# Matmuls on a constant tile in TensorE's waits of the first three attention items, and expert 1's weight split on ScalarE and VectorE

## The chip, the core and the metric

The kernel runs on one core of a Trainium2 chip. A core has TensorE (PE in the profile; its weight loads are PEld), VectorE (DVE), ScalarE (ACT), GpSimd (POOL) and SyncE (SP), each with its own instruction queue, and 16 DMA engines. The metric is the device time of one execution in microseconds; the number that counts is the median over several runs.

## The reference

Two parts in a row. Gated linear attention for 4 batches, 8 heads, 768 tokens, head size 48: `f = sigmoid(f_logit)`, and for every token `state = f * state + k (outer) v`, `y = q . state`. Its output is the input `x` (3072 tokens of 384) of a mixture of 8 experts with hidden size 1024:

```
P = np.exp(logits - logits.max())            # logits = x @ w_gate
for _ in range(8):
    P /= P.sum(1, keepdims=True) + 1e-09
    P /= P.sum(0, keepdims=True) + 1e-09
    P *= N / E
for e in range(E):
    out += P[:, e:e + 1] * (np.maximum(x @ w1[e], 0.0) @ w2[e])
```

Every token goes through every expert; the routing weights P need all logits, so all tokens, before they are known.

## The kernel before, in words

**Numbers.** Products are made in fp16 with each fp32 operand split in a high and a low half (names ending in h and l), so one product is three matmuls: high x high, high x low, low x high. A split is a cast to fp16 on ACT (the high half) and a subtraction on DVE or POOL (the low half).

**Stage 1, attention and raw experts (0 to about 420 us).** Attention is cut into 24 items of 128 tokens, 4 head pairs each. An item is a Python generator that yields between short groups of instructions. Its steps: load q, k and the gates (`q3`) and v (`vr`); sigmoid of the gates on ACT (`ft`); a reversed scan of their products on DVE (`r`); k times r (`km`); a second scan; q times it; high and low halves of k (`kb`), q (`qh`, `ql`) and v (`vh`, `vl`); k transposed (`ktp`, `kt`); scores (`aps`, masked into `am`, split into `ah`, `al`); outer products of k and v (`kvps`); the state (`st`, split into `sh`, `sl`) and the `carry` to the next item; the output (`yps`) and its split into the tokens `xh`, `xl`; and, two steps later, the gate logits (`lps`). An ordinary item (`item`, L615) transposes k by a DMA and uses POOL for q's product and k's low half. The first two (`early_item`, L495) transpose on PE and use DVE for both.

Between item steps PE runs a *filler*: experts 0 and 1 on tokens that are ready. For the first three blocks of 384 tokens it goes by tiles of 128 tokens (`moe_tile`, L417): twice 36 matmuls of 128 columns (`hps`), the halves `hh` on ACT and `hl` on DVE, then 24 matmuls of 384 columns (`yps`, the same name as the item's, told apart by its operands `w2h`, `w2l`). `raw_pairs` (L807) sets the order of tiles, expert 0 and expert 1 taking turns. `fill(n)` (L818) issues filler worth n units after each step of the loop; the table `FILL` gives n by step. One unit is one matmul of 384 columns, a third of one for 128. The loop over steps starts one new item every 8 steps, the first ordinary one `LEADS` steps in.

**Weights of experts 0 and 1.** `load` (L345) issues the DMA of one piece (4 of w1, 4 of w2 for each expert); later it splits it. Expert 0's pieces take one ACT operation (scale and cast, L360) and one on DVE (L362). Expert 1's go through `split_w` (L335): ACT scales in place (L340), ACT casts (L341), POOL subtracts (L342). Before the loop, a hand-written list of `go` and `fill` calls sets the order of item 0's steps, the loads and splits of expert 0, and the gate weights (`gate_weights`, L313).

**Stage 2, routing and conversion (about 420 to 514 us).** The filler goes on, 8 units a step. Beside it run the routing (`balance`, L941: 8 rounds of row and column sums on DVE with one small PE matmul `sk_c` a round) and the conversion of the tokens of each of 4 blocks to 15 sums and differences that the last stage multiplies (`convert`, L896; its casts on ACT, its subtractions on DVE). The next three conversions begin at steps 24, 48 and 64 of that loop (L1023); the last one's splits run on into the last stage.

**Stage 3, experts 2 to 7 (about 514 to 1563 us).** 48 periods of 15 slots (`period`, `SLOTS`). A slot is 6 matmuls into one of six PSUM banks `kb_A` to `kb_F`, with ACT copying (`cp`, L1164) and DVE adding (L1166, L1169) between them, and the second layer of the period before (`kyps`) fed in. A table `plan` holds side work by period and slot; among it the *checks* (`all_checks`, L1094): loads and maxima of all weights, then `guard` (L735) with samples of q, k (`qks`, 4 loads of 4 DMAs each) and v, then `verdict` (L775). Each call does one step of the checks, one to three of them a period.

**What sets the order.** `mm` (L278, its issue L279) chains all matmuls, so PE runs them in program order. `pin` (L270) chains an instruction behind the last pinned one of its engine. Nearly all work on DVE, ACT and POOL is pinned; the operations of `guard`, `verdict` and `partition_reduce` are not, so that the scheduler places them. SP issues DMAs in program order.

## Time and profile before

| what | value |
|---|---|
| runs (3), median | 1568.99 us |
| lowest, highest | 1566.51, 1572.23 us |
| the profiled execution's own time | 1571.83 us |
| its span in the trace | 1570.1 us |
| mean granted PE clock in it | 0.993 |
| PE busy | 1517.6 us (97%) |
| DVE busy | 1083.9 us (69%) |
| ACT busy | 780.4 us (50%) |
| POOL busy | 536.0 us (34%) |

The profile is of one execution. Matmuls overlap in it, so the time that one costs is the distance between the starts of two, not its own duration; a row may stand for several (x12). A wait names the engine and line that came last. PEclk or the clock column is the granted clock of PE as a share of full speed.

### The profile page before, as it was taken

How to read it: one execution, taken by the hardware profiler on the slowest of the kernel's cores; microseconds unless marked ns; L12 is line 12 of the kernel's file. 1: busy time of each engine (PE TensorE's matmuls, PEld its weight loads, DVE VectorE, ACT ScalarE, POOL GpSimd, SP SyncE). 2: the span in 40 equal slices, each digit the busy share in tenths (PEclk: the TensorE clock that was granted, in tenths of full speed). 3: DMA queues.
4: the chain of work that ended last, by engine and by line, in shares of the span. 5: the costliest groups of instructions: out<-in, count | busy, mean ns of one | idle time of the engine just before them, and what ended most of it. 6: DMA issues, size and time to landing. Idle time of an engine off the chain costs nothing.

```text
span 1570.1 us, 32383 instructions
## 1 busy us (share of the span) xinstructions
PE 1517.6 (97%) x13400; PEld 1107.5 (71%) x13400; DVE 1083.9 (69%) x1798; ACT 780.4 (50%) x1493; POOL 536.0 (34%) x668
## 2 busy tenths in 40 slices
PE   5799999999999999999999999999999999999998
PEld 4688886666655677777777777777777767777775
DVE  7687777887467866676767776666766675656654
ACT  5655555555334655554455554545444444445432
POOL 1643444343644512333333323223222222223211
PEclk9899999999999999999999999999999999999999
DMA  8355454542001212222222222121112220000011
GB/s 249 100 139 129 112 140 95 133 120 71 21 26 41 71 53 88 69 86 71 87 76 80 77 86 62 41 62 51 61 51 62 59 67 11 21 13 19 1 56 68
DMA packets 91501, 114.83 MB, mean 73 GB/s; under 512 B 52464, under 2 KB 68976, under 8 KB 91344
## 3 DMA queue, kind: packets, MB, share of 16 engines
q1 hardware_dynamic: 91344, 112.68, 25.3%
q8 instruction: 106, 1.74, 0.5%
q14 instruction: 51, 0.42, 0.1%
HBM read 88.41 MB, written 14.16 MB: 65 GB/s over the span
## 4 chain that ended last, share of the span: by engine, by line
PE 87%; DVE 6%; ACT 3%; DMA 1%; issue 1%; POOL 1%; SPq 0%; DVEq 0%; ACTq 0%; POOLq 0%
PE kyps L279 35%; PE yps L279 12%; PE hps L279 9%; PE kb_A L279 8%; PE kb_B L279 8%; PE kb_D L279 6%; PE kb_C L279 4%; PE kb_E L279 2%; PE kb_F L279 2%; PE kvps L279 1%; PE aps L279 1%; DVE hl L394 1%; DMA qks<-in_qkf_dram 1%; DMA vr<-in_vbd_dram 0%; ACT kb L647 0%
## 5 line engine op out<-in xcount | busy, mean ns | idle before, releaser
L1070 POOL TENSOR_TENSOR acc<-acc,yt 128x384 f32<-128x384 f32 x172 | 173.0, 1006 | 635.5 <-ACT yt L1069 635.5
L279 PE MATMUL kyps<-k2h,kh 128*128 128x384 f16 x1152 | 376.5, 327 | 0.0
L279 PE MATMUL kyps<-k2h,kl 128*128 128x384 f16 x1152 | 376.3, 327 | 0.0
L279 PE MATMUL kyps<-k2l,kh 128*128 128x384 f16 x1152 | 376.3, 327 | 0.0
L279 PEld LDWEIGHTS <-k1h 128*128 128x128 f16 x2880 | 281.4, 98 | 71.0 <-issue 0.2
L279 PEld LDWEIGHTS <-kh 128*128 128x128 f16 x2304 | 225.4, 98 | 104.5 <-issue 0.3
L1069 ACT ACTIVATE yt<-kyps,pes 128x384 f32<-128x384 f32 x172 | 99.8, 580 | 324.7 <-PE kyps L279 322.8
L279 PEld LDWEIGHTS <-k1l 128*128 128x128 f16 x1440 | 140.7, 98 | 69.2 <-issue 11.7
L1066 DVE SCALAR_TENSOR_TENSOR acc<-kyps,pes,acc 128x384 f32<-128x384 f32 x92 | 56.8, 618 | 171.8 <-PE kyps L279 171.8
L279 PEld LDWEIGHTS <-kl 128*128 128x128 f16 x1152 | 112.7, 98 | 44.8
L279 PE MATMUL yps<-w2l,hh 128*128 128x384 f16 x384 | 126.0, 328 | 5.1 <-POOL w2l L342 3.7
L1164 ACT ACTIVATE cp<-kb_A 128x512 f32<-128x512 f32 x144 | 86.0, 597 | 85.5 <-PE kb_A L279 83.6
L279 PE MATMUL yps<-w2h,hh 128*128 128x384 f16 x384 | 125.8, 328 | 2.6 <-ACT w2h L360 2.0
L279 PE MATMUL yps<-w2h,hl 128*128 128x384 f16 x384 | 125.9, 328 | 1.1 <-DVE hl L441 1.1
L279 PEld LDWEIGHTS <-w1h 128*128 128x128 f16 x1344 | 100.7, 101 | 36.5 <-ACT w1h L341 3.3
L1164 ACT ACTIVATE cp<-kb_B 128x512 f32<-128x512 f32 x144 | 87.0, 604 | 52.0 <-DVE kb_B L1166 52.0
L279 PEld LDWEIGHTS <-hh 128*128 128x128 f16 x768 | 74.6, 98 | 51.2 <-issue 6.4
L1169 DVE TENSOR_TENSOR cp<-kb_D,cp 128x512 f32<-128x512 f32 x144 | 98.9, 687 | 13.8 <-PE kb_D L279 12.8
L279 PE MATMUL hps<-xh,w1h 128*128 128x128 f16 (+1 forms) x672 | 86.3, 264 | 3.9 <-ACT w1h L341 3.0
L279 PE MATMUL hps<-xl,w1h 128*128 128x128 f16 (+1 forms) x672 | 86.4, 262 | 0.1
L394 DVE SCALAR_TENSOR_TENSOR hl<-hps,hh 128x384 f16<-128x384 f32 x80 | 43.9, 550 | 61.2 <-ACT hh L393 61.0
L279 PE MATMUL hps<-xh,w1l 128*128 128x128 f16 (+1 forms) x672 | 85.0, 261 | 0.0
(247 smaller groups left out, 3677.4 us busy)
## 6 DMA issues: line engine op xcount, KB each, us to landing
wm<-in_w_dram SPq DMA_DIRECT2D x64, 384.0 KB, 3.0
q<-in_qkf_dram SPq DMA_DIRECT2D x23, 672.0 KB, 5.1
vr<-in_vbd_dram SPq DMA_DIRECT2D x24, 384.0 KB, 3.6
ys<-yr SPq DMA_DIRECT2D x48, 192.0 KB, 2.3
k1r<-in_w_dram SPq DMA_DIRECT2D x24, 384.0 KB, 3.0
k2r<-in_w_dram SPq DMA_DIRECT2D x24, 384.0 KB, 3.0
yb<-ys SPq DMA_DIRECT2D x48, 192.0 KB, 2.3
out_dram<-acc SPq DMA_DIRECT2D x24, 192.0 KB, 1.9
```

The lines of the kernel that those rows point to most:

```text
L279: ins = (nc.tensor.transpose if transpose else nc.tensor.matmul)(**kw)
L394: held[0] = pin(nc.vector.scalar_tensor_tensor(out=tl, in0=ps, scalar=0.0, in1=th, op0=ALU.max, op1=ALU.subtract))
L1066: pin(nc.vector.scalar_tensor_tensor(out=y, in0=ps, scalar=p, in1=y, op0=ALU.mult, op1=ALU.add))
L1069: pin(nc.scalar.activation(out=yt, in_=ps, func=AF.Copy, scale=p))
L1070: pin(nc.gpsimd.tensor_tensor(out=y, in0=y, in1=yt, op=ALU.add))
L1164: pin(nc.scalar.activation(out=fresh(ev[2]), in_=bk, func=AF.Copy))
L1169: pin(nc.vector.tensor_tensor(out=fresh(ev[4]), in0=bk, in1=old, op=ALU.add if ev[2] == '+' else ALU.subtract))
```

## The change

Five things, in the order of the program.

1. **Early items.** `early_item` now makes items 0, 1 and 2 (ordinary items begin with number 3, `LEADS` 4 to 20). Its steps are shorter and in another order: the cast of v stands behind those of k and q, k's low half and q's low half have steps of their own, the output's matmuls go by operand (those that need only `vh` and `ah` first) in place of by head pair, and for items 1 and 2 the second chunk's transposes and outer products come ahead of them. At certain places `warm(n)` issues n matmuls of 512 columns of a constant tile (`ind`) by itself into a PSUM bank that nothing reads: 20 + 5 + 2 + 3 + 2 + 4 in item 0, 5 + 4 in items 1 and 2, 54 in all.
2. **Filler.** `raw_pairs` runs expert 0's three tiles of the first block, then expert 1's three, and takes turns only after that. `FILL` has seven rates in place of three.
3. **Weights.** All 8 pieces of expert 0 are requested ahead of item 1's data and of the gate weights. Expert 1's pieces are split like expert 0's: one ACT operation and one on DVE, at steps 18 to 22, while item 2 runs. `split_w` is gone, and with it POOL's part.
4. **Conversion.** Block 0's splits have one more step between them, the later conversions begin at steps 28, 48 and 62, and the last one's splits take every second slot of period 0.
5. **Checks.** The operations of `guard`, `verdict` and `partition_reduce` are pinned, and `guard` requests load n in the step in which it reduces load n - 1.

```diff
-LEADS = 4
-FILL = ((0, 6.5), (12, 6.3), (26, 9.1))
+LEADS = 20
+FILL = ((0, 12), (1, 4), (4, 6), (8, 0), (12, 6), (20, 9), (41, 8.6))
...
-        if e:
-            ws[e][k - 1].append(split_w(raw, e, j, k))
-            return
-        wh, wl = (wp0.tile(list(raw.shape), F16, name=f"w{k}{q}_0_{j}", tag=f"w{q}") for q in "hl")
+        wh, wl = ((wp1 if e else wp0).tile(list(raw.shape), F16, name=f"w{k}{q}_{e}_{j}", tag=f"w{q}") for q in "hl")
         scale = W1S if k == 1 else W2S
         pin(nc.scalar.activation(out=wh, in_=raw, func=AF.Copy, scale=scale))
         yield
         pin(nc.vector.scalar_tensor_tensor(out=wl, in0=raw, scalar=scale, in1=wh, op0=ALU.mult, op1=ALU.subtract))
...
+    def warm(n):
+        ps = bank([128, 512], f"wps{banks[0]}")
+        for _ in range(n):
+            mm(out=ps, lhsT=ind[:, 0:128], rhs=ind[:, 0:NB * C], start=True, stop=True)
...
+        if not i:
+            warm(20)
         transposed(0, 0)
+        yield
+        for rs, ks in heads:
+            pin(nc.vector.tensor_tensor(out=kb[rs, 1, :, ks], in0=km[rs], in1=kb[rs, 0, :, ks], op=ALU.subtract))
+        warm(5)
+        yield
+        pin(nc.vector.tensor_tensor(out=ql, in0=fl, in1=qh, op=ALU.subtract))
         transposed(1, 0)
+        if not i:
+            warm(2)
...
+        if i:
+            kv1 = outer(1)
+        warm(4)
...
-        for u in range(TILED):
+        for e in range(2):
+            for t in range(TT):
+                yield from moe_tile(e, 0, t)
+        for u in range(1, TILED):
             for t in range(TT):
                 for e in range(2):
                     yield from moe_tile(e, u, t)
...
+        at_steps(second[n], 4 + n, *((18, 18), (18, 18), (19, 19), (19, 19), (21, 21), (21, 21), (22, 22), (22, 22))[n])
...
+            if not b:
+                yield
...
-        if step in (24, 48, 64):
-            work.append(converts[{24: 1, 48: 2, 64: 3}[step]])
+        if step in (28, 48, 62):
+            work.append(converts[{28: 1, 48: 2, 62: 3}[step]])
...
-    at_slots(0, range(4, 15), converts[3])
-    at_slots(1, range(15), converts[3])
+    at_slots(0, range(4, 15, 2), converts[3])
+    at_slots(1, range(1, 15), converts[3])
```

and in `guard` (the loop over q, k and v in place of two loops):

```diff
+        for n in range(9):
+            now = (load_qk if n < 4 else load_v)(n % 4) if n < 8 else None
+            if before:
+                pin(nc.vector.tensor_reduce(out=before[1], in_=before[0], axis=AX.X, op=ALU.max, apply_absolute_value=True))
+            before = now
             yield
```

How the order of instructions moves is shown at three places. The first is SP's queue at the start. Names are tiles: `w1r_0_3` is the raw piece 3 of w1 of expert 0, `q3_1` and `vr_1` are item 1's data, `wgr` the gate weights. Before:

```order
L353 DMA w1r_0_3_169<-in_w1_dram 128x768
L315 DMA wgr_171<-in_wg_dram 128x384
L353 DMA w2r_0_0_173<-in_w2_dram 128x768
L353 DMA w2r_0_1_175<-in_w2_dram 128x768
L501 DMA q3_1_177<-in_qkf_dram 112x1536
L506 DMA vr_1_179<-in_vbd_dram 128x768
L353 DMA w2r_0_2_371<-in_w2_dram 128x768
```

After, in the same place:

```order
L343 DMA w1r_0_3_169<-in_w1_dram 128x768
L343 DMA w2r_0_0_171<-in_w2_dram 128x768
L343 DMA w2r_0_1_173<-in_w2_dram 128x768
L343 DMA w2r_0_2_175<-in_w2_dram 128x768
L343 DMA w2r_0_3_177<-in_w2_dram 128x768
L493 DMA q3_1_179<-in_qkf_dram 112x1536
L498 DMA vr_1_181<-in_vbd_dram 128x768
L315 DMA wgr_183<-in_wg_dram 128x384
```

Item 1's data stand behind two more w2 pieces, and the gate weights behind all of it.

The second is DVE's queue from item 1's first scan on (`r_1`; `w2l_0_2` is the low half of a piece of expert 0, `hl` a low half of the filler's hidden layer, `carry_0` item 0's state handed on). Before:

```order
L514 SCALAR_TENSOR_TENSOR r_1_459<-ft1_126,ind_103 112x512
L516 TENSOR_SCALAR pi1_127<-r_1_459 112x8
L517 RECIPROCAL pi1_127<-pi1_127 112x8
L362 SCALAR_TENSOR_TENSOR w2l_0_2_469<-w2r_0_2_371,w2h_0_2_468 128x768
L522 SCALAR_TENSOR_TENSOR q3_1_177<-q3_1_177,r_1_459 112x512
L523 SCALAR_TENSOR_TENSOR q3_1_177<-ft1_126,pi1_127 112x512
L362 SCALAR_TENSOR_TENSOR w2l_0_3_488<-w2r_0_3_373,w2h_0_3_487 128x768
L529 TENSOR_TENSOR q3_1_177<-q3_1_177 112x512
L534 TENSOR_TENSOR kb1_125<-q3_1_177,kb1_125 48x8x64 x2
L536 TENSOR_TENSOR ql_1_501<-q3_1_177,qh_1_500 112x512
L537 SCALAR_TENSOR_TENSOR vl1_139<-vr_1_179,vh1_133 128x768
L566 SCALAR_TENSOR_TENSOR am_1_581<-aps_1_535,mask_99 128x512
```

After:

```order
L506 SCALAR_TENSOR_TENSOR r_1_382<-ft1_126,ind_103 112x512
L508 TENSOR_SCALAR pi1_127<-r_1_382 112x8
L509 RECIPROCAL pi1_127<-pi1_127 112x8
L349 SCALAR_TENSOR_TENSOR w1l_0_2_354<-w1r_0_2_167,w1h_0_2_353 128x768
L428 SCALAR_TENSOR_TENSOR hl_0_0_0_0_425<-hps_0_0_0_0_387,hh_0_0_0_0_424 128x512
L512 SCALAR_TENSOR_TENSOR q3_1_179<-q3_1_179,r_1_382 112x512
L349 SCALAR_TENSOR_TENSOR w1l_0_3_361<-w1r_0_3_169,w1h_0_3_360 128x768
L543 TENSOR_TENSOR carry_0_462<-kvps_0_1_428,st_0_272 112x384
L517 SCALAR_TENSOR_TENSOR q3_1_179<-ft1_126,pi1_127 112x512
L520 TENSOR_TENSOR q3_1_179<-q3_1_179 112x512
L349 SCALAR_TENSOR_TENSOR w2l_0_0_467<-w2r_0_0_171,w2h_0_0_466 128x768
L318 SCALAR_TENSOR_TENSOR wgs_106<-wgr_183,wgs_106 128x3x8
```

Where two splits of expert 0 stood among item 1's steps, now six of its eight do, with a hidden half, the carry and the gate weights' split; item 1's `kb`, `ql`, `vl` and `am` follow further down, and expert 1's eight splits stand in item 2.

The third is DVE's queue around the reductions of the samples of q and k (`qkm`; `kb_34_A` is bank A of period 34). Before:

```order
L752 TENSOR_REDUCE qkm_17531<-qks1_17660 112x16
L1166 TENSOR_TENSOR kb_34_A_17200<-kb_34_A_17200,cp34_13_17244 128x512
L752 TENSOR_REDUCE qkm_17531<-qks2_17833 112x16
L1066 SCALAR_TENSOR_TENSOR acc1_8720<-kyps_33_0_1_17263,pes_114,acc1_8720 128x384
L1105 TENSOR_REDUCE wmx_115<-wm_2_7_3_17130 128x1
L777 TENSOR_REDUCE wg6_18724<-wmx_115 128x2
L778 TENSOR_REDUCE wg6_18724<-wmx_115 128x2
L783 TENSOR_SCALAR okm_156<-wg6_18724 128x1
L784 TENSOR_SCALAR okm_156<-wg6_18724 128x1
L1166 TENSOR_TENSOR kb_34_B_17218<-kb_34_B_17218,cp34_0_17316 128x512
L785 TENSOR_SCALAR okm_156<-wg6_18724 128x1
L752 TENSOR_REDUCE qkm_17531<-qks3_17916 112x16
```

After:

```order
L780 TENSOR_REDUCE qkm_17607<-qks1_17739 112x16
L1185 TENSOR_TENSOR kb_36_B_17829<-kb_36_B_17829,cp36_0_17929 128x512
L1085 SCALAR_TENSOR_TENSOR acc3_9327<-kyps_35_1_0_17918,pes_114,acc3_9327 128x384
L1185 TENSOR_TENSOR kb_36_C_17889<-kb_36_C_17889,cp36_9_17960 128x512
L1188 TENSOR_TENSOR cp36_2_17975<-kb_36_D_17953,cp36_6_17896 128x512
L1193 SCALAR_TENSOR_TENSOR kl_36_0_0_17802<-kb_36_A_17813,kh_36_0_0_17801 128x512
L780 TENSOR_REDUCE qkm_17607<-qks2_17912 112x16
L1185 TENSOR_TENSOR kb_36_D_17953<-kb_36_D_17953,cp36_7_17992 128x512
L1188 TENSOR_TENSOR cp36_10_18026<-kb_36_D_17953,cp36_1_17898 128x512
L1193 SCALAR_TENSOR_TENSOR kl_36_1_0_17808<-kb_36_B_17829,kh_36_1_0_17807 128x512
L1185 TENSOR_TENSOR kb_36_E_18019<-kb_36_E_18019,cp36_2_17975 128x512
L780 TENSOR_REDUCE qkm_17607<-qks3_17995 112x16
```

Two of the four reductions stood within a few operations of one another in period 34; now each stands at its check step, in period 36, with the period's own work between.

## The prediction

> **What bounds the kernel now.** I read four views: the page for the span, the windows by stage, the waits of TensorE (PE), and single rows of the timeline. The windows' columns are the stretch, then the busy time of PE, PE's weight loads, VectorE (DVE), ScalarE (ACT) and GpSimd (POOL), PE's granted clock, the DMA share and GB/s.

> ```profile
> span 1570.1 us, 32383 instructions
> PE 1517.6 (97%) x13400; PEld 1107.5 (71%) x13400; DVE 1083.9 (69%) x1798; ACT 780.4 (50%) x1493; POOL 536.0 (34%) x668
> ```
> ```profile
> 0.00:20.00 20.00, 7.07 (x89) 6.07 (x90) 12.79 (x37) 10.28 (x18) 5.34 (x14) 1.00 0.90 259
> 20.00:40.00 20.00, 13.85 (x144) 11.05 (x143) 16.55 (x29) 12.18 (x22) 1.07 (x2) 0.88 0.78 232
> 40.00:60.00 20.00, 13.10 (x159) 10.83 (x156) 12.61 (x16) 16.69 (x28) 13.99 (x10) 0.78 0.19 63
> 60.00:80.00 20.00, 16.89 (x217) 13.54 (x216) 12.37 (x17) 8.48 (x17) 11.32 (x10) 0.91 0.53 147
> 80.00:100.00 20.00, 18.78 (x310) 15.54 (x308) 19.67 (x31) 12.59 (x27) 9.49 (x10) 1.00 0.68 157
> 100.00:120.00 20.00, 18.89 (x330) 16.30 (x328) 14.73 (x23) 10.21 (x20) 10.15 (x9) 1.00 0.36 99
> 440.00:460.00 20.00, 16.84 (x106) 10.04 (x105) 16.50 (x37) 7.15 (x13) 10.58 (x17) 1.00 0.03 11
> 520.00:540.00 20.00, 17.48 (x136) 13.08 (x135) 18.74 (x34) 14.83 (x28) 11.05 (x16) 1.00 0.13 42
> 700.00:800.00 100.00, 100.00 (x748) 72.91 (x747) 70.76 (x112) 51.44 (x97) 34.90 (x46) 1.00 0.26 79
> 1200.00:1300.00 100.00, 96.30 (x711) 70.02 (x710) 66.63 (x114) 46.23 (x86) 30.28 (x48) 0.98 0.22 58
> ```

> PE is busy 1517.6 of 1570.1 us, so what can be won is 52.5 us of idle time and whatever PE runs below full clock. From 120 us on PE is full but for a few places. In the first 120 us it is busy 7.07 + 13.85 + 13.10 + 16.89 + 18.78 + 18.89 = 88.6, so idle 31.4. The clock columns of 20 to 80 us (0.88, 0.78, 0.91 of 20 us each) take another 2.4 + 4.4 + 1.8 = 8.6. The clock column says 1.00 at the start, but rows show half speed there (start, duration, matmuls in the row; matmuls overlap, so I use differences of starts):

> ```profile
> 18.78 1.81 PE L279 MATMUL hps<-xh,w1h 128*128 128x128 f16 x12 [0.85 <-ACT xh L600]
> ...
> 25.32 0.86 PE L279 MATMUL hps<-xh,w1l 128*128 128x128 f16 x12
> ```

> The chain of waits has the same kinds at full speed, later on (start, us on the chain, matmuls); the yps x13 are an expert's, of 384 columns, the yps x48 an item's:

> ```profile
> 97.84 2.12 PE yps L279 x13
> 99.95 0.84 PE hps L279 x15
> 100.79 0.70 PE aps L279 x24
> 101.49 1.02 PE kvps L279 x24
> ...
> 109.91 0.14 PE lps L279 x6
> ...
> 112.99 1.43 PE yps L279 x48
> ```

> At full speed an hps takes 0.84 / 15 = 0.056 and an expert's yps 2.12 / 13 = 0.163. The first 60 hps take 6.54 (18.78 to 25.32) where 60 x 0.056 = 3.35: 3.2 lost. Item 0's attention matmuls before that, at half speed, lose at most another 3 (0.70 + half of the kvps + 36 of the 48 yps + transposes); I take 2. Lost in all to 120 us: 31.4 + 8.6 + 3.2 + 2 = 45.

> **The change part by part.** *Early items.* The waits of PE in the first 130 us (engine, line, releaser: us in total, times, longest):

> ```profile
> PE ktp L279 <- ACT kb L527: 10.8, 1, 10.8
> PE yps L279 <- POOL w2l L342: 3.7, 3, 1.6
> PE hps L279 <- ACT w1h L341: 3.0, 2, 2.6
> PE yps L279 <- DVE sl L583: 2.0, 1, 2.0
> ```

> The change removes 6.7 us of these: the POOL subtractions of expert 1's weights and the ACT steps ahead of them go, since expert 0 now runs three tiles alone before expert 1 is touched. The first 10.8 stay for real work; the 20 warm matmuls lie inside them. What they change is PE's clock, not what it waits for. PE runs in program order, so a warm matmul stands between two real ones and ends before the second is released, or delays it. The 54 (512 columns each) cost at full speed, scaled from the 0.163 of 384 columns, 0.217 each, 0.43 at half: the 20 end before item 0's first transpose is ready, the other 34 (7.3 to 14.7 us) lie mostly in waits.

> Useful work up to the third tile's end: a tile is 72 x 0.056 + 24 x 0.163 = 7.9, so 23.8; an item is 0.70 + 1.02 + 1.43 + 0.14 = 3.3, three 9.9; transposes about 0.8 an item, 2.4, minus 0.4 for item 0's shorter yps. Together 35.7. So the question is when the third tile ends, and for that the new bound of the stage is DVE, which takes the splits from POOL:

> ```profile
> L441 DVE SCALAR_TENSOR_TENSOR hl<-hps,hh 128x512 f16<-128x512 f32 x7 | 4.8, 685 | 13.2 <-ACT hh L440 13.2
> L362 DVE SCALAR_TENSOR_TENSOR w2l<-w2r,w2h 128x768 f16<-128x768 f32 x4 | 3.8, 947 | 1.5 <-ACT w2h L360 1.5
> L534 DVE TENSOR_TENSOR kb<-q,kb 48x512 f16<-48x512 f32 x4 | 2.7, 684 | 1.4 <-ACT kb L527 1.3
> L523 DVE TENSOR_TENSOR_SCAN q<-ft,pi 112x512 f32<-112x512 f32 x2 | 2.4, 1218 | 0.0
> ```

> An ACT group of the same stretch, and the load of item 1 (KB, us from issue to landing):

> ```profile
> L440 ACT ACTIVATE hh<-hps 128x512 f16<-128x512 f32 x8 | 4.7, 592 | 8.5 <-PE hps L279 8.5
> ```
> ```profile
> q<-in_qkf_dram SPq DMA_DIRECT2D x1, 672.0 KB, 11.2
> ```

> In program order DVE has from its first scan (r of item 0) to the sixth hl (third tile) 8 scans x 1.22, 16 splits x 0.95, 6 hl x 0.69, and some 30 operations of the attention with 384 to 768 columns that the rows price at 0.55 to 0.95: about 60 us, of which 13 belong to item 0 and stand before item 1's scan. That scan waits for item 1's load. In before this transfer, issued at 8.59, takes 11.2 and is there at 19.8. In after two more w2 pieces are ahead of it in SP's queue and the gate weights behind, 0.6 MB more at the 259 and 232 GB/s of these stretches: 2.5 us later, 22.3 (between the 19.8 of before and some 24, if the stretch moves no more than 150 GB/s). From there 60 - 13 = 47 us of DVE work, 2.4 for the gate weights' split (six ACT operations of about 0.55 stand ahead of the cast that it needs, less the 0.95 of the split ahead of it on DVE), 6 for waits of DVE on PE and ACT (bounds 0 and 13.2, the first row's idle time), and the last half of the 24 yps, 2: the third tile ends at 22.3 + 47 + 2.4 + 6 + 2 = 80, with waits of item 2's own chain say 82. Lost till then: 82 - 36 = 46, and I keep 1 of the 2.3 that PE idles from 80 to 120 now. So 47 against 45: **+2**, bounds -5 (DVE waits nothing, load at 20) and +8 (13 us of waits).

> How long a wait must be to halve PE's clock decides whether warm matmuls matter, and what rival C below is worth:

> ```profile
> 36.00:38.00 2.00, 0.42 (x5) 0.18 (x2) 1.99 (x4) 1.18 (x2) 0.00 (x0) 0.50 0.37 97
> ```
> ```profile
> 35.25 0.48 PE L279 MATMUL yps<-w2h,hh 128*128 128x384 f16 x1 [2.02 <-ACT w2h L360]
> ```

> The granted clock is 0.50 from 36 on, after a wait of 2.02. So waits of about 2 us are enough here, and C keeps its chance. [...]

> *Item 2 on PE.* 16 more transposes and their copies: the 0.8 above, real work that before has as a DMA transpose; DVE takes over item 2's q product and kb-lo from POOL, in the count above. **+0.8** (0 to 1.5).

> *Filler rate.* FILL spends about 39 units (of 0.163 us) less in stage 1. They are run in stage 2 instead, where they hide the routing. No matmul is lost, **0** as long as PE stays full from 120 to 420; if a rate of 8.6 to 9 units a step leaves an item's chain too little time, the existing yps wait (row L704 below) grows: up to +2.

> *Stage 2, routing and conversion.* Waits of PE after 130 us:

> ```profile
> PE kb_D L279 <- DVE cp L1169: 4.2, 3, 3.4
> PE sk_c L279 <- DVE sk_cs L128: 3.8, 4, 2.7
> ...
> PE yps L279 <- DVE sl L704: 2.0, 3, 1.1
> ```

> The routing's column sums wait 3.8 in all (window 440 to 460: 16.84 of 20), behind conversion splits on DVE. The change adds a step between item block 0's splits and starts the later conversions at steps 28, 48, 62, so a routing step has at most one split ahead of it; and 39 more units lie there. **-1.5**, bounds -3.2 and 0. At the junction (520 to 540, 2.5 idle) the last conversion's splits are spaced into every second slot of period 0 and 4 or 5 small check operations of DVE (0.6 us each at most) go to later slots: **-1**, bounds -2.5 and +1, since the splits now stand among the period's own DVE work.

> *Checks pinned.* Before, the reductions over samples of q and k are not pinned; the order shows four of them bunched, and each waits for its own load:

> ```profile
> DVE qkm L752 <- DMA qks<-in_qkf_dram: 7.3, 4, 3.8
> ```

> DVE stands 7.3 us there, and kb_D, queued behind on DVE, keeps PE 3.4 (row kb_D). The clock falls after it: 711 matmuls in 1200 to 1300 against 748 in 700 to 800, 37 x 100/748 = 5.0 us. After, the load is issued a check step before its reduction, three slots or more of a period's 15 (48 periods take the 1050 us of the last stage, so three slots are 4.4 us), against the 3.8 of the longest wait in the row: little or none is left. **-5**, bounds -3 (idle alone) and -5.

> Sum: +2 + 0.8 + 0 - 1.5 - 1 - 5 = -4.7. Against the profiled execution, 1571.8 (span 1570.1 and 1.7 around it), 1567.1; that execution is 2.8 above the median of the runs, 1569.0, so the median is forecast at **1564.3**.

> **The rivals.** *A, clearly faster.* DVE waits little in the first items and item 1's load lands at 20: the third tile ends at 82 - 6 - 2.3 = 74 to 76 and the early term is -5. For it: POOL's slow subtractions are gone, and with them what they cost DVE while both run. Sum -5 + 0.8 - 1.5 - 1 - 5 = -11.7: 1557.

> *B, no change.* The check term comes, but the early items lose what stage 2 gains: third tile at 85 (DVE waits 9), +5, and the routing and junction terms 0 (another wait ends last in their place). Sum +5 + 0.8 - 5: 1570; with half of these, 1567. For it: the routing wait has three causes in a row, and only the split ahead of it is moved.

> *C, slower: half clock through three tiles.* The warm matmuls are issued behind the waits, not in them: PE in order cannot fetch one while a real matmul waits. If each of the waits of expert 0's three tiles is above the 2.02 us that was seen to halve the clock, the 216 hps and 72 yps run at half, 216 x 0.056 + 72 x 0.163 = 24 us more, half of it under waits anyway: +12, the third tile ends at 92 to 94. Then the sum is +12 + 0.8 - 1.5 - 1 - 5 = +5: 1574. It decides from a third tile later than 91. Against it: the change feeds 4 to 12 units a step through the waits.

> *D, the change doesn't do what it says*: the 20 matmuls leave the clock as it is. It gives the same as the forecast, since that puts the start of item 1's chain on the load.

> **How the numbers follow.** Forecast (with D) 0.42, A 0.22, B 0.24, C 0.12. About 0.3%, 4.7 us, is what a measurement of this kernel can tell from no change: faster is below 1564.3, slower above 1573.7. The forecast stands on the bound: half of it (0.21), all of A (0.22) and a little of B (0.04, by its better half) give 0.47 for faster; C 0.12 slower; 0.41 for the rest. The range takes the forecast's own bounds, A to 1555 (all terms at their better ends but one) and B whole, to 1573; most of C and the far end of A, 2 in 10 together, are left out.

> **What would show it.** Right: the sk_c row falls under 2 us, the qkm row is gone, and 1200 to 1300 has 745 matmuls or more; the third tile's last yps at 80 to 84; item 1's load in at 22. Wrong: a third tile past 90 or a clock under 0.8 in 40 to 80 (C); PE waits at 130 to 420 above 4 us (filler rate); a DVE wait on qks after all; a new wait of kb_A to kb_F in period 0 or 1 above 3 us (the splits at the junction).

## The result, and the profile after

The changed kernel takes 1581.72 us (median of 4 runs, 1581.05 to 1582.34); the kernel before took 1570.61 beside it (4 runs, 1566.51 to 1572.27). The ratio is 1.0075, 95% interval 1.0052 to 1.0097: 0.75% slower, where 0.3% faster was forecast. The medians differ by 11.1 us, the two profiled executions by 9.2, and the places below are read from these two:

```profile
span 1579.3 us, 32525 instructions
PE 1530.6 (97%) x13470; PEld 1109.5 (70%) x13470; DVE 1089.0 (69%) x1810; ACT 776.5 (49%) x1489; POOL 516.8 (33%) x656
```

The windows of the changed kernel, the same stretches as before and one more, 1400 to 1500:

```profile
0.00:20.00 20.00, 16.41 (x153) 9.24 (x154) 14.30 (x39) 12.50 (x23) 5.32 (x14) 1.00 0.92 293
20.00:40.00 20.00, 13.06 (x138) 9.15 (x136) 15.97 (x25) 8.87 (x16) 1.81 (x2) 0.74 0.68 206
40.00:60.00 20.00, 13.73 (x210) 11.47 (x208) 12.03 (x20) 9.20 (x19) 1.34 (x2) 0.83 0.35 110
60.00:80.00 20.00, 14.29 (x181) 10.28 (x178) 17.84 (x27) 14.03 (x25) 3.44 (x3) 1.00 0.09 30
...
520.00:540.00 20.00, 16.46 (x118) 11.95 (x117) 17.75 (x28) 14.82 (x26) 6.96 (x10) 0.91 0.17 56
1200.00:1300.00 100.00, 100.00 (x753) 73.53 (x752) 66.48 (x109) 48.71 (x91) 31.84 (x49) 1.00 0.18 48
...
1400.00:1500.00 100.00, 95.02 (x700) 68.06 (x698) 55.51 (x93) 43.31 (x81) 21.87 (x28) 1.00 0.03 11
```

and the last of them in the kernel before:

```profile
1400.00:1500.00 100.00, 100.00 (x753) 73.20 (x750) 60.53 (x106) 44.57 (x84) 21.85 (x28) 1.00 0.04 15
```

Two rows tell most of it. 1200 to 1300 went from 711 matmuls to 753: the wait for the samples of q and k is gone, as forecast. 1400 to 1500 went from 753 to 700: a larger loss where there was none, at a place the prediction did not look at.

To sort the rest, I took two things from the timeline of PE. For the last stage, a period's length, from its first matmul on bank A to that of the next. For the stages ahead, how much is lost: the time at which a matmul starts, less the full-speed cost of all matmuls ahead of it in program order, at the prices of the prediction (the constant-tile matmuls count as nothing).

| place | before | after | difference, us |
|---|---|---|---|
| lost up to item 5's scores | 47.0 | 47.6 | +0.6 |
| lost from there to the routing's first matmul | 2.9 | 3.6 | +0.7 |
| lost from there to period 0 | 5.9 | 7.7 | +1.8 |
| work ahead of period 0 (item 2's transposes) | 457.1 | 458.0 | +0.9 |
| periods 0 and 1 | 13.25 + 22.72 | 11.79 + 25.92 | +1.7 |
| period 34 | 27.22 | 21.59 | -5.6 |
| periods 41 to 46, together | 130.5 | 139.1 | +8.6 |
| the other periods, and after the last matmul | | | +0.5 |

The other 39 periods agree to 0.3 us each, most to 0.01, so a difference of one profile against another is sharp there. It is not in the first 100 us (see the last section).

Where 1400 to 1500 loses is in the waits of PE, 1398 to 1540, in the changed kernel (before, PE waits there for kb_A alone, 0.6 in two waits):

```profile
PE kyps L279 <- DVE acc L1085: 2.1, 3, 0.7
PE kyps L279 <- ACT yt L1088: 2.1, 3, 0.7
PE kyps L279 <- DVE gd_r L99: 1.0, 2, 0.6
```

These waits count idle time only. From start to start, the stalled `kyps` take 8.4 us longer than others of their kind, which is the whole of the +8.6 in the table. The second layer's matmuls (`kyps`) wait for the engine that empties the tile before, which normally has a whole tile's time for that, since two banks take turns. What is new there is the verdict: five transposes of a column (`gd_t`) that DVE then reduces (`gd_r`). The view of those tiles, changed kernel (first and last start stand behind the durations):

```profile
L279 PE MATMUL gd_t<-identf,wg x5: 272/273/273, 1403.6 to 1497.5; 128*1 128x128 f32 x5
L99 DVE TENSOR_REDUCE gd_r<-gd_t x5: 269/269/270, 1416.3 to 1510.2; 1x1 f32<-1x128 f32 x5
```

and the kernel before:

```profile
L279 PE MATMUL gd_t<-identf,wg x5: 272/273/273, 1396.3 to 1483.3; 128*1 128x128 f32 x5
L99 DVE TENSOR_REDUCE gd_r<-gd_t x5: 266/268/279, 1397.1 to 1484.1; 1x1 f32<-1x128 f32 x5
```

Taken one by one, the five were reduced 0.3 to 1.3 us after their transposes before, 3.5 us in all; now it is 3.8 to 20.4 us, 64.7 in all. `gd_t` comes from the pool `psm`, two banks with tag `m`, and so do the `kyps`. In `partition_reduce` a `yield` stands between transpose and reduction. Unpinned, the scheduler had put the reduction right behind its transpose, whatever the program's order; pinned, it goes where the program has it, one check step later. All that time one of the two banks is taken.

### The profile page after: what moved, and what is told of

It reads as the page before. It is cut to its first block, busy times and chain, and to the rows that moved or that the text cites. A ratio compares the mean times of both kernels' runs of the same rounds, so it can differ in the third digit from the quotient of the medians.

```text
span 1579.3 us, 32525 instructions
## 1 busy us (share of the span) xinstructions
PE 1530.6 (97%) x13470; PEld 1109.5 (70%) x13470; DVE 1089.0 (69%) x1810; ACT 776.5 (49%) x1489; POOL 516.8 (33%) x656
## 4 chain that ended last, share of the span: by engine, by line
PE 86%; DVE 7%; ACT 3%; issue 2%; DMA 1%; POOL 1%; SPq 0%; ACTq 0%; DVEq 0%; POOLq 0%
PE kyps L279 35%; PE yps L279 12%; PE kb_B L279 8%; PE kb_A L279 8%; PE hps L279 7%; PE kb_D L279 6%; PE kb_C L279 4%; PE kb_E L279 2%; PE kb_F L279 2%; PE kvps L279 1%; DVE hl L381 1%; PE aps L279 1%; DMA vr<-in_vbd_dram 1%; ACT yt L1088 0%; DMA w1r<-in_w_dram 0%
## 5 line engine op out<-in xcount | busy, mean ns | idle before, releaser
L279 PE MATMUL kyps<-k2h,kh 128*128 128x384 f16 x1152 | 375.9, 326 | 5.8 <-DVE acc L1085 2.1
L279 PE MATMUL kyps<-k2l,kh 128*128 128x384 f16 x1152 | 375.9, 326 | 0.0
L279 PE MATMUL kyps<-k2h,kl 128*128 128x384 f16 x1152 | 375.9, 326 | 0.0
L279 PEld LDWEIGHTS <-k1h 128*128 128x128 f16 x2880 | 281.6, 98 | 70.7 <-issue 0.2
L279 PEld LDWEIGHTS <-kh 128*128 128x128 f16 x2304 | 225.6, 98 | 104.3 <-issue 0.3
L279 PEld LDWEIGHTS <-k1l 128*128 128x128 f16 x1440 | 140.7, 98 | 66.0 <-issue 9.0
L279 PEld LDWEIGHTS <-kl 128*128 128x128 f16 x1152 | 112.8, 98 | 53.4 <-issue 9.4
L279 PE MATMUL yps<-w2h,hl 128*128 128x384 f16 x384 | 126.0, 328 | 4.1 <-DVE hl L428 3.7
L279 PE MATMUL yps<-w2l,hh 128*128 128x384 f16 x384 | 126.1, 328 | 0.0
L279 PE MATMUL yps<-w2h,hh 128*128 128x384 f16 x384 | 125.9, 328 | 0.0
L279 PEld LDWEIGHTS <-w1h 128*128 128x128 f16 x1344 | 97.6, 98 | 35.2 <-issue 4.4
L279 PEld LDWEIGHTS <-hh 128*128 128x128 f16 x768 | 74.9, 98 | 46.2 <-issue 1.3
L279 PE MATMUL hps<-xl,w1h 128*128 128x128 f16 (+1 forms) x672 | 84.6, 257 | 2.1 <-DVE xl L618 1.7
L279 PE MATMUL hps<-xh,w1h 128*128 128x128 f16 (+1 forms) x672 | 84.1, 259 | 0.9 <-DVE hl L381 0.8
L279 PE MATMUL hps<-xh,w1l 128*128 128x128 f16 (+1 forms) x672 | 84.0, 257 | 0.0
L279 PE MATMUL kb_A<-xbh,k1h 128*128 128x256 f16 x288 | 78.5, 273 | 0.8 <-ACT yr L398 0.6
## 6 DMA issues: line engine op xcount, KB each, us to landing
q<-in_qkf_dram SPq DMA_DIRECT2D x23, 672.0 KB, 5.2
```

The source lines that it names most:

```text
L279: ins = (nc.tensor.transpose if transpose else nc.tensor.matmul)(**kw)
```

## The experiments

Twelve kernels. Where one time is given, it is a single run, and the verdict rests on the periods and waits of its profile, not on the time alone.

**gd_unpinned.** The changed kernel, one edit:

```diff
-    pin(nc.vector.tensor_reduce(out=row, in_=ps[0:1, :], axis=AX.X, op=op))
+    nc.vector.tensor_reduce(out=row, in_=ps[0:1, :], axis=AX.X, op=op)
```

> The changed kernel with one edit: the five partition reductions of the verdict are not pinned, so that DVE takes each as soon as its transpose is there, as before. Theory (a bank is held): a transpose of the verdict sits in one of the two PSUM banks that the second layer's tiles use, until its reduction; pinned, that stands a whole check step later, 12.7 us in the first case, and the second layer has one bank meanwhile. Then periods 41 to 46, 8.7 us longer in the changed kernel than in the kernel before, go back to 21.6 to 22.0 us each and the time falls by 8 to 9, to about 1573. Rival (the 1400s are lost to something else in the changed checks: the pinned small operations, a later tail): less than 3 us comes back, 1579 or more.

Measured: 1573.21 (before beside it 1571.35). Periods 41 to 45 are 21.7 to 21.8 each, all others as in the changed kernel. The theory holds in place and in size.

**gd_same_step.** Pinned, but in the step of its transpose:

```diff
     mm(transpose=True, out=ps[0:1, :], in_=col, identity=identf)
     row = pool.tile([1, 1], F32, name=name + "_r")
-    yield
     pin(nc.vector.tensor_reduce(out=row, in_=ps[0:1, :], axis=AX.X, op=op))
+    yield
     return row
```

> The changed kernel with the reduction of each verdict transpose pinned in the same check step as its transpose, not the next one. Theory (a bank is held): the bank is free after about a slot, 7 to 9 us come back, about 1573. Rival (pinning itself costs, since DVE in order waits for PE's transpose and everything on DVE stands behind it): the loss stays or grows, 1581 to 1585.

Measured: 1572.95. The stretch is whole again:

```profile
1400.00:1500.00 100.00, 100.00 (x752) 73.26 (x751) 60.19 (x100) 45.02 (x85) 22.21 (x28) 1.00 0.05 15
```

So pinning is not what costs; the time between the two instructions is. DVE does wait for PE's transposes now, 3.5 us in four waits, and PE's matmuls lose nothing by it.

**gd_hold_twice.** The bank held two steps:

```diff
     row = pool.tile([1, 1], F32, name=name + "_r")
     yield
+    yield
     pin(nc.vector.tensor_reduce(out=row, in_=ps[0:1, :], axis=AX.X, op=op))
...
             rows.append((yield from partition_reduce(nc, cst, psm, "m", identf, g[:, col:col + 1], op, f"gd{n}", mm, pin)))
-            yield
```

> The changed kernel with the bank held twice as many check steps: transposes and reductions stand two steps apart in place of one, with no free step between one pair and the next, so the number of steps is the same. Theory (a bank is held): the price goes with the time it is held, 8.7 us more, 1588 to 1592. Rival (a fixed price for each of the five, whatever the time held): the same as the changed kernel, 1580 to 1583.

Measured: 1587.89, 6.2 over the changed kernel, just under the range of the theory. Waits of PE from 1390 on:

```profile
PE kyps L280 <- ACT yt L1088: 6.5, 9, 0.7
PE kyps L280 <- DVE acc L1085: 3.5, 5, 0.7
```

Six tiles waited in the changed kernel on `yt` or `acc`, 14 wait here, still 0.7 each. Periods 41 to 46 take 146.9 together, 7.8 more than in the changed kernel and 16.4 more than before, and the banks are held 124.5 us in place of 64.7. So both the price and the time held are 1.9 times those of the changed kernel: the price goes with the number of second-layer tiles that fall into the time a bank is held. The rival of a fixed price is out. (The two profiled executions, 1581.05 and 1587.89, lie 6.8 apart: the first items and the end took 0.9 less in the second.)

**no_warm.** The 54 matmuls on the constant tile left out:

```diff
-        for _ in range(n):
+        for _ in range(0):
             mm(out=ps, lhsT=ind[:, 0:128], rhs=ind[:, 0:NB * C], start=True, stop=True)
```

> The changed kernel without the 54 matmuls on the constant tile; all else the same. Theory (DVE's chain of scans and splits sets the pace of the first three items; what the warm matmuls change is PE's clock between its waits): the loss up to item 5 stays within 2 us of the 47.6 measured, the third tile ends at 83 or up to 2 later; 1581 to 1584. Rival (the warm matmuls keep the clock up and carry the early stage): the clock in 0 to 60 us falls well below and the loss grows by 4 us or more, over 1585. Other rival (they stand in the way): the loss falls by 2 or more.

Measured: 1582.31, inside the changed kernel's own runs. Lost up to item 5: 49.0, against 47.6 in the changed kernel and 46.0 to 48.3 over five other kernels here with the same first three items. So the headline edit is worth about 1 us, less than these differ among themselves.

The first 20 do raise the clock, which the clock column can't show, since it reads 1.00 from 0 to 20 in both kernels. Item 0's 24 matmuls for the scores in the changed kernel, and what follows them:

```profile
12.21 0.22 PE L279 MATMUL aps<-qh,kb 112*128 112x64 f16 x2
...
12.91 0.28 PE L279 MATMUL kvps<-vh,kt 128*112 128x96 f16 x2
```

and in `no_warm`:

```profile
10.30 0.32 PE L279 MATMUL aps<-qh,kb 112*128 112x64 f16 x2
...
11.82 0.40 PE L279 MATMUL kvps<-vh,kt 128*112 128x96 f16 x2
```

They take 0.70 us there and 1.52 here, about half speed. But item 0 starts 2 us later for it, with more constant-tile matmuls between its steps, and item 1's first outer product is issued at 20.55 with them and at 20.42 without: by then nothing is left of the gain. From 20 to 60 the clock moves less than one would think. In `no_warm`:

```profile
0.00:20.00 20.00, 10.00 (x117) 8.77 (x118) 14.46 (x39) 11.95 (x21) 5.31 (x14) 1.00 0.92 291
20.00:40.00 20.00, 11.51 (x114) 7.85 (x112) 15.20 (x22) 9.37 (x16) 1.82 (x2) 0.67 0.64 193
40.00:60.00 20.00, 12.97 (x175) 11.07 (x173) 11.94 (x20) 8.29 (x17) 1.35 (x2) 0.82 0.31 104
```

0.67 and 0.82 from 20 to 60, against 0.74 and 0.83. The waits stand where the constant-tile matmuls do not: these are issued behind a real matmul that waits, as after the longest wait of the changed kernel here, where five of them then run at half clock (0.50 from 30.9 to 33.3):

```profile
30.75 0.23 PE L279 MATMUL lps<-wgs,xh 128*128 128x16 f16 x3 [4.21 <-DVE wgs L318]
...
30.91 2.29 PE L279 MATMUL wps<-ind 112*128 112x512 f16 x5
```

**warm_10.** `gd_same_step` with `warm(10)` for `warm(20)`.

> gd_same_step with 10 matmuls in the first block in place of 20. In the changed kernel the 20 end at 10.3 us, in no_warm item 0's first transpose ran at 8.2. Theory (the block is too long and holds item 0 back, but item 1's chain, which waits for DVE, hides it): item 0's first transpose at 8.2 to 8.6, at most 1 us less in the loss up to item 3, 1572 to 1574. Rival (item 0's start is passed on to the third tile): 1.5 to 2 us less in the loss up to item 3.

Measured: 1573.15; lost up to item 5 47.8 against 48.0. The first block's rows in the changed kernel, and the row it delays:

```profile
2.98 0.61 PE L279 MATMUL wps<-ind 112*128 112x512 f16 x1 [2.98 <-DVE ind L307]
...
10.31 0.36 PE L279 MATMUL ktp<-identh,kb 112*128 112x112 f16 x4
```

In `no_warm` the same transpose:

```profile
8.24 0.53 PE L279 MATMUL ktp<-identh,kb 112*128 112x112 f16 x4 [8.24 <-ACT kb L515]
```

Twenty take 7.3 us and end 2 us after item 0 could go on. With ten, item 0's transpose starts at 8.25, and the third tile's last yps is issued at 83.1, against 83.6 in `gd_same_step` and 82.7 in the changed kernel: item 1's chain, on DVE and its loads, hides both the delay and its removal.

**before_new_checks.** The kernel before with the changed `guard` and `verdict` alone, and the reduction in its own step as in `gd_same_step`:

> The kernel before with only the changed checks (guard and verdict pinned, loads requested a step ahead) and with each verdict transpose reduced in its own check step, so that no bank is held. Theory (the five gains and losses add: the wait for the samples of q and k goes, worth 5.6 us in period 34, and nothing else moves): 5 to 6 us faster than before, about 1565. Rival (period 34 is short in the changed kernel only because of its other parts): within 1 us of before.

Measured over five runs: 1565.48 (1564.31 to 1566.66) against 1570.44; ratio 0.9965, interval 0.9952 to 0.9979. Period 34 is 21.60 and

```profile
1200.00:1300.00 100.00, 100.00 (x753) 73.39 (x751) 64.83 (x106) 47.44 (x90) 29.95 (x49) 1.00 0.17 42
```

The forecast's term of -5 is real, and stands alone.

**before_pin_only.** The same, but with `guard`'s loops as they were and only `pin(...)` around each operation.

> The kernel before with guard and verdict pinned but guard's loops as they were (load n requested just after the reduction of load n - 1), each verdict transpose reduced in its own check step. Theory (what made DVE wait was the place the scheduler gave the unpinned reductions, not the moment of the loads): the same gain, 5 to 6 us, about 1565. Rival (the earlier request is what counts): DVE still waits for qks and 2 to 5 us of the gain are missing, 1567 to 1570.

Measured: 1566.59, period 34 at 21.59. Pinning is enough; the earlier request adds nothing that shows.

**same_step_old_convert.** `gd_same_step` with the conversions as before:

```diff
-            if not b:
-                yield
...
-        if step in (28, 48, 62):
-            work.append(converts[{28: 1, 48: 2, 62: 3}[step]])
+        if step in (24, 48, 64):
+            work.append(converts[{24: 1, 48: 2, 64: 3}[step]])
...
-    at_slots(0, range(4, 15, 2), converts[3])
-    at_slots(1, range(1, 15), converts[3])
+    at_slots(0, range(4, 15), converts[3])
+    at_slots(1, range(15), converts[3])
```

> The changed kernel with the reductions in the same step (gd_same_step, 1573.0) and with the conversions as before: no extra step in block 0, starts at 24, 48 and 64, the last one's splits in every slot from 4 of period 0 and 0 of period 1. Theory (the spread of the splits costs at the junction and gives little to the routing): periods 0 and 1 fall from 37.7 to 36.0 us, and the routing stage, which lost 7.7 against 5.9 before, goes back by 1 to 2: 2 to 4 us less, 1569 to 1571. Rival (the longer routing stage comes from the work moved there by the filler's rate, not from the conversions): only the junction's 1.7 come back or less, and the routing's waits grow, 1571 to 1574.

Measured: 1570.94. The routing stage lost 6.1 in place of 7.6, as the theory had it. The junction did not come back: period 0 went from 11.79 to 13.45, and period 1 stayed at 25.95, which takes away what the routing gave; the 2.0 us between the two times are the first items' scatter (46.0 lost there, not 48.0, with the same instructions). So the slots of the last conversion are not what makes period 1 long, and the theory's reading of the junction fell.

**late_splits.** `gd_same_step` with the last conversion kept out of period 0:

```diff
-    at_slots(0, range(4, 15, 2), converts[3])
-    at_slots(1, range(1, 15), converts[3])
+    at_slots(1, range(4, 15), converts[3])
+    at_slots(2, range(15), converts[3])
```

> gd_same_step (1573.0) with the last conversion's splits held out of period 0: they start at slot 4 of period 1, about where they ran in the kernel before. Theory (39 more filler units in the routing stage let the last conversion get ahead, so its splits fall into period 0, where ACT and DVE are tight, and the copy of bank A that PE needs in period 1 comes late, 2.5 us with a halved clock behind it): period 1 falls from 25.9 to 22.7 us or less, period 0 stays near 11.8, about 1570. Rival (period 1 is long for another reason): period 1 stays above 25, 1573.

Measured: 1570.28; period 0 at 11.79, period 1 at 22.50 (25.91 without the edit). Waits of PE, 517 to 575, in `gd_same_step`:

```profile
PE kb_A L279 <- ACT cp L1183: 2.7, 2, 2.5
```

and in `late_splits`:

```profile
PE kb_A L279 <- ACT cp L1183: 1.0, 2, 0.8
```

Before, the last conversion was still adding in period 0 and cast in period 1. In `gd_same_step` its casts (0.84 us on ACT) and subtractions (0.95 on DVE) begin in period 0, at 526.5, and run on into the first slots of period 1: one of DVE's stands there ahead of its addition to bank F, ACT casts bank F after that, and the copy of bank A that PE needs next is queued behind that cast. Behind PE's wait of 2.5 the clock is at 0.50 for 3.4 us, from 534.7 on (the changed kernel has the same: a wait of 2.55 up to 534.16, then 0.50 from 534.75 to 538.16), which is 1.7 of the 3.2 us that period 1 lost; in `late_splits`, where the longest wait on that copy is 0.8, period 1 is 3.4 us shorter. That the casts come early because the routing stage is longer is argued, since no run set the filler's rates back: of the filler, 1738 units stand ahead of the last item's gate logits before and 1687 after, so 51 move into the routing stage (the prediction had 39), which is six steps of 8.

**same_step_pool_split.** `gd_same_step` with expert 1's low halves on POOL:

```diff
-        pin(nc.vector.scalar_tensor_tensor(out=wl, in0=raw, scalar=scale, in1=wh, op0=ALU.mult, op1=ALU.subtract))
+        if e:
+            pin(nc.scalar.activation(out=raw, in_=raw, func=AF.Copy, scale=scale))
+            pin(nc.gpsimd.tensor_tensor(out=wl, in0=raw, in1=wh, op=ALU.subtract))
+        else:
+            pin(nc.vector.scalar_tensor_tensor(out=wl, in0=raw, scalar=scale, in1=wh, op0=ALU.mult, op1=ALU.subtract))
```

> gd_same_step (1573.0) with expert 1's low halves subtracted on POOL as before (ACT casts, ACT scales in place, POOL subtracts), at the changed kernel's steps. Theory (DVE sets the pace of the first three items, so the eight splits that it took over cost there): the third tile ends 2 to 5 us before 83, the loss up to item 5 falls by as much, 1568 to 1571. Rival (POOL's work slows DVE, 1846 ns in place of 692 for ql in the kernel before, and ACT has eight operations more): no gain, or 1 to 4 us slower, 1573 to 1577.

Measured: 1576.51, 3.6 slower; lost up to item 5 51.6. The theory of DVE as the only pace-maker fell. ACT, with eight operations more, is busy 17.65 of 20, and DVE, with eight fewer, 10.04:

```profile
60.00:80.00 20.00, 14.57 (x175) 10.17 (x173) 10.04 (x17) 17.65 (x29) 11.14 (x8) 0.93 0.03 11
```

and PE's longest new wait is 4.0 for ACT's `hh`. At these steps the split on DVE is the better one.

**before_checks_convert.** `before_new_checks` with the extra step in block 0 and the starts 28, 48 and 62.

> before_new_checks (1565.5) with block 0's splits one step further apart and the next conversions begun at 28, 48 and 62, the last one's splits in their old slots. In before_new_checks one column sum of the routing waits 2.65 us behind these splits and PE's clock is at half for three more us. Theory (the extra step clears that wait): 2 to 4 us less, 1561.5 to 1563.5. Rival (as in the changed kernel, where the routing's waits came to 3.2 in place of 3.8, the wait only moves to other rounds): within 1 us of 1565.5.

Measured over seven runs: 1565.99; ratio to before 0.9972 (0.9961 to 0.9983). The routing stage lost 4.3 in place of 8.4, a little more of a gain than the theory had; 1.7 of it is a stretch at half clock that the kernel before did not have either (last section). Then period 0 took 15.30 (12.47) and period 1 23.30 (22.72), with this row:

```profile
516.47 0.27 PE L279 MATMUL kb_A<-xbh,k1h 128*128 128x256 f16 x1 [3.11 <-ACT cp L1173]
```

ACT's copy waits for DVE, which is busy without a gap from 504 to 515 with additions and splits of the last two conversions. What PE gains in the routing it meets again at the junction.

**combined.** `before_new_checks` with the extra step and starts 28, 46 and 64.

> before_new_checks with block 0's splits one step further apart, and the next conversions begun at 28, 46 and 64 (24, 48 and 64 before), slots as before. In before_checks_convert the routing stage lost 4.1 us less than in before_new_checks, but the third conversion's splits then stood in a bunch in front of the last stage, and periods 0 and 1 took 3.4 us more. Theory (POOL is idle from 460 to 480 us, and a third conversion that starts two steps earlier has its splits done in the routing stage): the routing keeps its gain and periods 0 and 1 stay near 12.5 and 22.7, so 3 to 4 us less than before_new_checks, about 1562. Rival (DVE and POOL are full from 490 to 515, so what PE gains in the routing it gives back at the junction whatever the start): within 1 us of 1565.5.

Measured over five runs: 1565.97 against 1571.26; ratio 0.9964 (0.9951 to 0.9978). Periods 0 and 1 are 13.00 and 22.72 and the routing's sums wait 1.5 us in place of 3.8, but PE now waits 1.2 earlier in the junction, on a hidden half on ACT:

```profile
502.38 0.34 PE L279 MATMUL yps<-w2h,hh 128*128 128x384 f16 x1 [1.19 <-ACT hh L393]
```

Within the scatter this equals `before_new_checks`; the rival holds. The three versions with the new checks, at 1565.5 to 1566.0, are 5 us better than the kernel before and 16 better than the changed one.

## Why the prediction was wrong

The step that failed is the one on the checks, and within it the sentence that ended the working there. It priced the reductions of the samples, and took "pinned" as an edit with one consequence: no wait on a load. That consequence came, -5.6 for -5. But the same edit pins `partition_reduce`, which has a resource across its `yield`: a PSUM bank that the second layer needs. That was to be read in the code before any run, since `psm` has two buffers and `kyps` and `gd_t` share its tag, and in the order of instructions, which shows the five reductions move behind a check step's worth of other DVE work. I showed the order for the samples only. The term is +8.6, shown by four runs (unpinned, same step, held twice, and the checks alone).

Between the forecast's -4.7 and the +9.2 of the profiles lie 13.9 us. The checks make 8.0 of them (-5 said; -5.6 and +8.6 measured), the routing 3.3 and the junction 2.7; the small rest cancels. So without the held bank the change would still have been no gain: `gd_same_step` stands at 1572.95, the kernel before beside it at 1571.35.

Point by point, against the terms:

- *Early items, +2.* The end of the chain came where it was said, the third tile's last yps at 82.7 for 82, in part by luck. Item 1's load landed at 18.9 (said 22.3) and its scan starts at 20.1, and DVE then waits 14.2 us in the 60 to the end of its part, where 2.4 and 6 were said; PE alone waits 4.2 for the gate weights' split. The 60 us of DVE work do not come out of the parts given (46 to 58); 58.3 were measured. Measured +0.6 in the one pair of profiles; over six profiles with the new start and five with the old, 47.5 against 45.7 lost at item 5, +1.8.
- *The 20 constant-tile matmuls end ahead of item 0's transpose*: wrong by 2 us, and without weight, since item 1's chain sets the end. That they leave the clock as it is (rival D) is wrong too (item 0's scores take 0.70 us with them, 1.52 without), with as little weight.
- *Item 2's transposes, +0.8*: 0.9.
- *Filler rate, 0 to +2*: +0.7 in the stage itself. Its other effect, on when the last conversion runs, was not seen.
- *Routing, -1.5*: the waits for column sums fell from 3.8 to 3.2 only, and new ones came behind DVE's `hl` at 498 and 508: +1.8 in all. `same_step_old_convert` puts 1.5 of it on the conversions' steps.
- *Junction, -1*: period 0 did gain 1.5, period 1 lost 3.2. The sign was wrong for a reason in the list of edits: the conversion was thought to be spread by its slots, when its place in time counts, as `late_splits` shows, and that moves with the number of steps of the routing stage.
- *Rival C* (slower by half clock in three tiles) had the right sign and came nearest, with 1574, 7.7 short, for a mechanism that was not there: the third tile did not end after 91.

What stays open: which of the edits to the first items costs the 1.8 us there, how the 0.7 us between item 5 and the routing divides among the filler's rates, and the rest of the 1.8 in the routing stage. No run here separates them.

## What to carry to other kernels

When an operation is pinned, look at what it releases, not only at what it waits for: if a buffer is taken in one step and released in another, pinning turns the scheduler's freedom into holding time, and whoever shares the pool pays per tile (0.7 us for each tile that waited here). Put the release in the step of the claim. And where stages follow one another on helper engines that are full at the seam, a step won in one stage can be given back at the next (in `before_checks_convert`, 4.1 us won in the routing, 3.4 lost in periods 0 and 1): compare the stages' lengths, not the waits, before you count a gain.

## What the runs showed of the hardware

```profile
448.09:451.50 3.41, 2.34 (x15) 1.18 (x13) 3.34 (x6) 0.98 (x2) 3.41 (x5) 1.00 0.00 0
451.50:454.91 3.41, 1.83 (x12) 1.22 (x13) 3.22 (x10) 0.00 (x0) 3.33 (x6) 1.00 0.00 0
454.91:458.32 3.41, 3.41 (x23) 2.05 (x21) 2.69 (x6) 0.49 (x1) 2.88 (x7) 1.00 0.04 16
```

and `before_new_checks`:

```profile
448.83:452.24 3.41, 1.31 (x9) 0.92 (x10) 3.26 (x9) 0.00 (x0) 3.34 (x6) 1.00 0.00 0
452.24:455.65 3.41, 3.41 (x13) 1.59 (x12) 3.18 (x7) 0.00 (x0) 3.16 (x7) 0.50 0.00 0
```

An edge splits the wait in the kernel before, and no stretch has more than 1.58 us of idle PE; in `before_new_checks` 2.10 fall into one stretch, and the next is at half. Over all 14 profiles, each of the 51 full-clock stretches with 1.97 us of idle time or more is followed by one at half, 4 of the 63 with 1.0 to 1.92, and none with less. So the prediction's "about 2 us" is right for the idle time in such a stretch, and not for the length of a single wait.

The stretch at half makes 1.7 us of difference between two sums, for nothing in the code. What sets the edges, no run here shows.

**A scan of DVE took 3.2 us longer beside two subtractions on POOL.** In `same_step_pool_split`, a scan of DVE that takes 1.22 us elsewhere in the same profile takes 4.42 beside two subtractions of POOL, 3.24 us together: 1.22 + 3.24 = 4.46. A hidden half, one of whose two inputs is in PSUM, takes 0.69 beside two more such subtractions (75.37 to 78.62), as it does at 60.37 without them.

```profile
60.37 0.69 DVE L432 SCALAR_TENSOR_TENSOR hl<-hps,hh 128x512 f16<-128x512 f32 x1 [2.69 <-ACT hh L431]
...
77.42 0.69 DVE L432 SCALAR_TENSOR_TENSOR hl<-hps,hh 128x512 f16<-128x512 f32 x1 [2.33 <-ACT hh L431]
...
79.09 4.42 DVE L661 TENSOR_TENSOR_SCAN q<-ft,pi 112x512 f32<-112x512 f32 x1
...
95.22 1.22 DVE L661 TENSOR_TENSOR_SCAN q<-ft,pi 112x512 f32<-112x512 f32 x1
```
```profile
79.19 3.24 POOL L351 TENSOR_TENSOR w2l<-w2r,w2h 128x768 f16<-128x768 f32 x2
```

Why the scan takes longer and the hidden half does not, no run here shows.

**The first 100 us scatter.** Over five profiles with the old start and six with the new one, each with the same instructions up to item 3, the time lost by then ran from 43.5 to 45.7 and from 46.0 to 48.3, mostly with the time at which the first loads land: in the two groups item 1's load landed first, at 16.4 and 18.7 us, in the profile that lost least. A term of 1 or 2 us in that stage can't be read from one pair of profiles, whereas in the last stage 0.1 us can.
